# Attention into a Mish MLP on one core: weight loads by a second engine, products two slots behind, and new constants

## The chip, the cores and the metric

The kernel runs on 1 core of one Trainium2 chip. The metric is device time in microseconds (us) of one execution, and less is better. The kernel before took 982.59 us in the median of three runs (983.8, 977.85 and 982.59).

## The reference

Attention with a local window, and an MLP on what comes out of it:

```python
B, H, Sl, D = 8, 8, 512, 64      # batches, heads, local rows, head size; Sg = 32 global rows
k_all = concat([k_g, k_l]); v_all = concat([v_g, v_l])
out_g = sm(scale * q_g @ k_all.T) @ v_all              # global rows see all
s_ll = where(|row - col| <= 32, scale * q_l @ k_l.T, -1e9)
out_l = sm(concat([scale * q_l @ k_g.T, s_ll])) @ v_all
x = concat([out_g, out_l]) as rows                      # 8 * 544 = 4352 rows of 512
h = x @ w_in                                            # 512 x 2048
g = h * tanh(softplus(h))                               # Mish
return g @ w_out                                        # 2048 x 512, float32
```

## The kernel before

**The work.** Every large product is made of 16-bit floats: an operand is split into a high and a low half, and three products (high by high, high by low, low by high) stand for one.

The attention is cut into 128 *units*, one for each batch, pair of heads and quarter of the local rows; a name such as U_3_1 is batch 3, pair 1. A unit's scores `s` (line L616, TensorE) are masked and their row maxima taken by VectorE (L630), ScalarE makes the exponentials (L639) and the high half of them `ph` (L337), VectorE the low half (L659). A DMA transpose `pt<-ph` (L504, issued by SyncE) turns them, and twelve matmuls make the product `U` with the values (`va`, `vc`; L712). VectorE divides by the sums (`x`, L720 to L722), and from batch 1 on the rows are split (`xs`) and turned by DMA into `xh` and `xl`, the MLP's input; in batch 0 TensorE does the turning. Every pair of heads also has a small set of instructions for the 32 global rows (`g`, `gP`, `gu`, ...).

The MLP takes 256 rows at a time: 17 *blocks* (two for each batch, and the global rows), each of 8 *steps* i. A step makes `h` (24 matmuls, L848), Mish in ScalarE (L891), its halves `G` in VectorE (L339, L904), and adds to the output tiles `o_0` and `o_1` (six matmuls each, L916). After the eighth step ScalarE or VectorE scales `o` into `ob` (L337, L339), and a DMA stores it. PSUM holds 2 `h`, 2 `o`, 3 `s` and 1 `U`: the first `o` of a block needs the `ob` of the block before it.

**The weights** come as 64-bit floats: 32 loads of 512 KB, `w0` to `w15` for the first matrix, `w16` to `w31` for the second, all issued by GpSimd (L406, L409). VectorE makes 32-bit floats of each in three instructions (L422, L429, L431). Their scale (`w_norm`) needs all sixteen of a matrix, and then ScalarE and VectorE split each row of tiles (`W`); the second matrix's low halves are VectorE's (L493).

**The values** of a batch are one load of 1024 KB (`vraw`, one buffer). VectorE takes their maxima (`vmx`, L516 to L522), GpSimd reduces over partitions (L527), VectorE makes the scale `sv` (L531 to L535), and ScalarE and VectorE the halves (`vgf`, `vf`), which eight small DMAs of SyncE's for each pair of heads put into `va` and `vc`.

**The order.** Nothing is in program order. `slot(u)` records the tasks of unit u and of the MLP steps that the tables give to this slot; a task's place in the record is its priority (`BOOST` makes the MLP's later by that many places). The planner `Plan.order` then simulates all engines with costs of its own, each engine takes the ready task of the best priority, and that simulated order is what each engine's instructions are written in. So a constant's change reorders all engines. The constants that matter here: `BLOCKS` (slots at which the blocks 0 to 3 start), `LAGX` (how many slots each later step lies behind its number), the weights' `CONV`, `RATE`, `FIRST`, `STEP` and `AHEAD_DMA` (slots of the conversions, splits and loads).

Of the kernel before, what the change touches and what calls it, by code (L numbers as in the profile page):

```python
# [21 lines left out]
RED = bass_isa.ReduceOp  # L22
# [27 lines left out]
class Plan:  # L50
# [7 lines left out]
    LOYAL = 800  # L58
    TABLE = 1283
    COLD = 2  # L60
    DEEP, ISSUE, LANES = 4, 1000, 8

    def __init__(self):
        self.tasks = []
# [70 lines left out]
    def order(self):  # L135
        N = len(self.tasks)
        left, users = [0] * N, [[] for _ in range(N)]
        for n, t in enumerate(self.tasks):
            both = t[2] | t[3]
            left[n] = len(both)  # L140
            for d in both:
                users[d].append(n)
        free = dict.fromkeys((PE, DVE, ACT, POOL, DMA), 0)
        queue = {e: [] for e in free}
        start, done, on = [None] * N, [0] * N, [None] * N
        columns = {}
# [19 lines left out]
        def first(e):  # L166

            best = None
            for pri, n, ns, t in queue[e]:
                table = self.tasks[n][7]  # L170
                t = max(t, free[e])
                if table == "dma":
                    t = max(t, far[-self.DEEP] if len(far) >= self.DEEP else 0, soft[-self.LANES] if len(soft) >= self.LANES else 0)
                elif e == DMA:
                    t = max(t, hard[-self.LANES] if len(hard) >= self.LANES else 0)
                elif e == ACT and table not in (None, self.table):
                    t += self.TABLE
                e0 = self.tasks[n][0][0][0]
                if e0 != e and free[e0] <= t + self.LOYAL:
                    continue  # L180
                if best is None or t < best[0]:
                    best = (t, pri, e, n, ns)
                    if t == free[e]:
                        break
            return best
# [3 lines left out]
                enter(n)  # L189
        for _ in range(N):  # L190
            t, pri, e, n, ns = min(c for c in map(first, free) if c)
            start[n], on[n] = t, e
            if self.tasks[n][7] == "dma":
                s = max(t + self.DMA_IN, late)
                both = min(ns, max(0, moved + self.DMA_IN - s))
                moved += both
                late = s + ns + both
                far.append(late)
                free[e] = t + self.ISSUE
                done[n] = far[-1] + self.DMA_OUT  # L200
                soft.append(done[n])
                queue[e] = [c for c in queue[e] if c[1] != n]
                for u in users[n]:
                    left[u] -= 1
                    if not left[u]:
                        enter(u)
                continue
            if e == ACT:
                self.table = self.tasks[n][7] or self.table
            for x, _ in self.tasks[n][0]:  # L210
                queue[x] = [c for c in queue[x] if c[1] != n]
            if e == PE:
                ns = tensor(t, ns, self.tasks[n][6]) - t
            if e == DVE and free[POOL] > t:
                ns += 0.6 * min(ns, free[POOL] - t)
            if e == DMA:
                s = max(moved, t)
                both = min(ns, max(0, late - s - self.DMA_IN))
                late += both
                moved = s + ns + both  # L220
                free[e] = max(t + max(self.DMA_MIN, self.tasks[n][6]), moved - self.DMA_AHEAD)
                done[n] = moved + self.DMA_IN + self.DMA_OUT
                hard.append(done[n])
            else:
                free[e] = done[n] = t + ns
            for u in users[n]:
                left[u] -= 1
                if not left[u]:
                    enter(u)
# [15 lines left out]
def attn_mish_kernel(ctx: ExitStack, tc: tile.TileContext, qt, kt, vm, vg, qg, w1, w2, consts_in, out, w64):  # L245
# [76 lines left out]
    def dma(kib):  # L322
        return kib * 2.81
# [41 lines left out]
    def wkeys(k):  # L365
        if k < 16:
            return [[("W", k // 4 * 2 + 1 + g), k % 4] for g in range(2)]
        j, hf = HV[k]
        return [[("W", j + j // 8 + 1), hf]]
# [20 lines left out]
    def rawkey(k):  # L390
        return ("W", PLACE[k]) if PLACE[k] in range(18) else ("wraw", k)

    def word(k, w):
        x = raw(k).rearrange("p (f w) -> p f w", w=2)[:, :, w]
        return x.rearrange("p (g f) -> p g f", g=2) if k < 16 else x

    def w_load(k):
        j, hf = HV[k]

        def go():  # L400
            n = 2 if w64 else 1
            dst = raw(k) if w64 else wf(k).bitcast(I32)
            if k < 16:
                c, f0 = k % 4, k // 4 * 512 * n
                src = w1[c * 128:(c + 1) * 128, f0:f0 + 512 * n]
                G.dma_start(dst, src if w64 else src.rearrange("p (g f) -> p g f", g=2))  # L406
            else:
                r0 = (j - 8) * 256 + hf * 128
                G.dma_start(dst, w2[r0:r0 + 128, :])  # L409
        if w64:  # L410
            p = PLACE[k]
            pl.add(POOL, dma(512), go, w=[rawkey(k)] if p in range(18) else (), new=() if p in range(18) else [(p, ("wraw", k))], table="dma")
        else:
            pl.add(POOL, dma(256), go, w=wkeys(k), table="dma")

# [526 lines left out]
    UNITS.sort(key=lambda x: (x[0], x[2] // 2, x[1], x[2]) if x[0] < HALVED else x)  # L944
    steps = [(blk, i) for blk in range(NBLK) for i in range(NF)]

    BLK2 = 28.778
    BLK3 = 44.139
    LAGX = 17.0
    BLOCKS = [9, 17, max(25, int(BLK2)), max(33, int(BLK3))]  # L950
    PACE = 0.762
    S1 = [int(BLOCKS[s // NF] + PACE * (s % NF)) if s < 4 * NF else s + max(17, int(LAGX)) for s in range(len(steps))]
    LAG2 = 2
    BOOST = 78.591

    def at(u):
        return [x for x, v in zip(steps, S1) if v == u]
# [1 line left out]
    def unit(u):  # L959
        return UNITS[u] if 0 <= u < NU else None  # L960
# [3 lines left out]
    def slot(u):  # L964
# [4 lines left out]
            pl.slot = None  # L969

        m, m2, md = (at(u - k) for k in (0, LAG2, LAG2 + 1))
        fu, bu, vu = unit(u + 1), unit(u), unit(u - 1)
        b, hp, t = bu if bu else (0, 0, -1)
        n1, n3 = divmod(b * HP + hp + 1, HP), divmod(b * HP + hp + 3, HP)
        load3 = bu and b >= HALVED and HALVED < n3[0] < B
# [18 lines left out]
        for x in md:  # L994
            if x[1] == NF - 1:
                store(x[0])
        if mv1 and t == 1:
            v_hi(*n1)
        pl.late = BOOST
        for x in m[:1]:  # L1000
# [27 lines left out]
        if t == 2:  # L1028
            g_exp(b, hp)
            g_norm(b, hp)  # L1030
            g_turn(b, hp)
        if mv1 and t == 1:
            v_lo(*n1)
        pl.late = BOOST
        for x in m2:
# [13 lines left out]
        if vu and vu[0] < HALVED and vu[2] == 3:  # L1049
            k_load(vu[0] + 1, vu[1])  # L1050
            q_load(vu[0] + 1, vu[1])
        if mv1 and t == 1:
            v_move(*n1)
        if vu and vu[2] == 3 and (vu[0] < HALVED - 1 or vu[:2] == (HALVED - 1, 0)):
            v_parts(vu[0] + 1, vu[1])
# [12 lines left out]
        if bu and HALVED <= b < B - 1:  # L1068
            if hp == 2 and t == 1:
                b_load(b + 1)  # L1070
                g_load(b + 1)
            if hp == 2 and t >= 2:
                for k in ((0, 1), (2, 3, 4))[t - 2]:
                    b_max(b + 1, k)
            if hp == 2 and t == 3:
                b_scale(b + 1)
            if hp == 3 and t == 0:
                b_split(b + 1)


# [1 line left out]
    ORDER = "k0 q0 m w0 b w1 w2 k1 q1 w3 w4 k2 q2 w5 w6 k3 q3 w7 w8 w9 w10 g w11 w12 w13 w14 w15"  # L1082
    LOAD1 = -7.335
    LOADS1 = 0.0
    CONV1 = 0.623
    RATE1 = 0.077
    CONV2 = 3.656
    RATE2 = 0.645
    FIRST1 = 7.58
    STEP1 = 0.746  # L1090
    FIRST2 = 7.262
    STEP2 = 0.393
    AHEAD_DMA = 13.043

    def weights():
        for k in range(32):
# [15 lines left out]
        pl.settle()  # L1112

    V.memset(pmax, 0.0)
    pl.add(POOL, 6000, lambda: G.partition_all_reduce(warm, pmax, 128, RED.max))
    for i, x in enumerate(ORDER.split()):
        a, n = x[0], int(x[1:] or 0)
        pl.slot = LOAD1 + LOADS1 * i
# [18 lines left out]
    weights()  # L1137
    splits += [(FIRST1 + STEP1 * j, j) for j in range(8)] + [(FIRST2 + STEP2 * j, 8 + j) for j in range(8)]
    splits.sort()
    for u in range(-1, max(S1[-1] + LAG2 + 2, NU + 2)):  # L1140
        slot(u)
    with tc.manual_schedule(engines={E.PE, E.DVE, E.Activation, E.Pool, E.SP}):
        pl.emit()
# [55 lines left out]
```

## Time and profile before

| | |
|---|---|
| runs | 983.8, 977.85, 982.59 us; median 982.59 us |
| profiled execution | 984.26 us, span 982.3 us |
| TensorE busy (matmuls) | 920.9 us, 94% of the span |
| VectorE, ScalarE busy | 570.0 us and 573.5 us, 58% each |
| GpSimd busy | 29.8 us |
| mean granted TensorE clock | 0.982 |
| DMA | 113.74 MB, mean 116 GB/s |

The span runs from the first to the last instruction; the execution's own time has 1.96 us around it. Engines are PE (TensorE), DVE (VectorE), ACT (ScalarE), POOL (GpSimd) and SP (SyncE, which issues most DMAs). A clock of 1.00 is 2.4 GHz, of 0.50 it is 1.2 GHz. A row such as "9.5, 8, 1.9" in the view of the waits gives the total, the count and the longest wait.

### The profile page before, as it was taken

To read this page: it belongs to the slowest core of one execution; us is meant where nothing else is said; L and a number is where in the kernel's file an instruction comes from. 1 tells how busy PE (TensorE), PEld (TensorE's weight loads), DVE (VectorE), ACT (ScalarE), POOL (GpSimd) and SP (SyncE) were. 2 spreads that over 40 slices of the span, in tenths; PEclk is the share of its full clock that TensorE was granted. 3 is DMA by queue.
4 is the path that set the end of the run, shared out by engine and by line. 5 is a ranking of instruction groups with operands and counts; after the bars stand their busy time and mean duration, and the time that the engine had idled before them with its cause. 6 is when DMAs were issued, how large, how long until landed. Compare 5 with 4: busy or idle time off the path is not lost.

```text
span 982.3 us, 20578 instructions
## 1 busy us (share of the span) xinstructions
PE 920.9 (94%) x8044; PEld 627.1 (64%) x8044; DVE 570.0 (58%) x1747; ACT 573.5 (58%) x1181; POOL 29.8 (3%) x57
## 2 busy tenths in 40 slices
PE   2678899999899879999999999999999999999997
PEld 1456556767566556667676667666666666666664
DVE  4799886667477554766566655665565553322222
ACT  2266876778578556767676767676776753211111
POOL 6201000000000000000000000000000000000000
PEclk9689999999999999999999999999999999999999
DMA  9874225676677844567356555646362333000000
GB/s 360 299 220 135 87 62 135 125 148 150 157 147 148 176 119 103 119 149 146 84 132 144 122 105 125 154 88 132 93 121 48 83 63 62 22 1 22 1 22 22
DMA packets 214417, 113.74 MB, mean 116 GB/s; under 512 B 181168, under 2 KB 194608, under 8 KB 213296
## 3 DMA queue, kind: packets, MB, share of 16 engines
q1 hardware_dynamic: 209568, 95.39, 43.6%
q0 software_dynamic: 4608, 16.78, 4.8%
q8 instruction: 63, 1.03, 0.4%
q14 instruction: 34, 0.28, 0.1%
q10 hardware_dynamic: 144, 0.26, 0.1%
HBM read 46.32 MB, written 8.91 MB: 56 GB/s over the span
## 4 chain that ended last, share of the span: by engine, by line
PE 77%; DMA 7%; DVE 7%; ACT 5%; SPq 1%; issue 1%; POOL 1%; ACTq 0%; DVEq 0%; POOLq 0%
PE h L848 31%; PE o L916 31%; PE s L616 5%; PE U L712 4%; DMA pt<-ph 3%; PE g L750 2%; DMA vraw<-in_vm 1%; PE gu L804 1%; PE rest L487 1%; ACT L891 1%; DVE W L429 1%; DVE W L431 1%; DMA va<-vgf 1%; ACT P L639 1%; DVE G L904 1%
## 5 line engine op out<-in xcount | busy, mean ns | idle before, releaser
L916 PE MATMUL o<-W,G 128*128 128x512 f16 x1632 | 388.7, 380 | 5.3 <-ACT ob L337 5.3
L848 PE MATMUL h<-xh,W 128*128 128x256 f16 x2048 | 376.2, 273 | 2.5 <-ACT W L330 2.5
L848 PEld LDWEIGHTS <-W 128*128 128x128 f16 x3264 | 310.0, 98 | 69.5 <-issue 9.3
L848 PE MATMUL h<-xl,W 128*128 128x256 f16 x1024 | 279.7, 273 | 0.0
L916 PEld LDWEIGHTS <-G 128*128 128x128 f16 x1632 | 156.3, 98 | 155.9 <-issue 10.3
L891 ACT ACTIVATE e<-h,c 128x512 f32<-128x512 f32 (+1 forms) x137 | 92.4, 684 | 161.9 <-PE h L848 137.4
L339 DVE TENSOR_SCALAR G<-e,c 128x512 f16<-128x512 f32 x135 | 64.8, 482 | 169.4 <-ACT e L891 168.2
L639 ACT ACTIVATE P<-P,nm 128x192 f32<-128x192 f32 (+1 forms) x256 | 117.4, 459 | 63.2 <-DVE nm L630 61.6
L904 DVE SCALAR_TENSOR_TENSOR G<-e,c,G 128x512 f16<-128x512 f32 (+1 forms) x137 | 101.7, 745 | 3.4
L630 DVE CUSTOM_DVE_ANT_0 P<-s,consts 128x192 f32<-128x192 f32 (+1 forms) x256 | 86.1, 368 | 27.8 <-PE s L616 24.5
L712 PEld LDWEIGHTS <-pt 96*128 96x128 f16 (+1 forms) x1536 | 61.0, 98 | 40.3 <-DMA pt<-ph 14.9
L891 ACT ACT_TABLE_LOAD x65 | 83.4, 1283 | 1.1
L659 DVE SCALAR_TENSOR_TENSOR ph<-P,ph 128x384 f16<-128x384 f32 (+1 forms) x112 | 63.7, 588 | 30.9 <-ACT ph L337 28.6
L712 PE MATMUL U<-va,pt 128*128 128x64 f16 (+1 forms) x768 | 56.7, 194 | 18.4 <-DMA pt<-ph 9.5
L616 PE MATMUL s<-k,q 64*128 64x192 f32 (+1 forms) x512 | 66.2, 375 | 4.9 <-DMA q<-in_qt 4.6
L337 ACT ACTIVATE ph<-P 128x384 f16<-128x384 f32 (+1 forms) x107 | 54.9, 537 | 12.7 <-DMA pt<-ph 12.2
L616 PEld LDWEIGHTS s<-k,q 64*128 64x128 f32 x512 | 44.3, 194 | 22.5 <-issue 14.8
L712 PE MATMUL U<-vc,pt 96*128 96x64 f16 x768 | 56.0, 194 | 0.0
L772 ACT ACT_TABLE_LOAD x25 | 32.1, 1283 | 40.4 <-DVE gmx L767 40.3
L639 ACT ACT_TABLE_LOAD x40 | 51.3, 1283 | 0.7
L639 ACT ACTIVATION_READ_ACCUMULATOR P<-P,nm 128x1 f32 x256 | 47.8, 187 | 0.0
L337 ACT ACTIVATE ob<-o,c 128x512 f32<-128x512 f32 (+1 forms) x34 | 22.8, 669 | 29.4 <-PE o L916 29.4
(116 smaller groups left out, 714.1 us busy)
## 6 DMA issues: line engine op xcount, KB each, us to landing
k<-in_kt SPq DMA_DIRECT2D x32, 320.0 KB, 3.6
wraw<-in_w POOLq DMA_DIRECT2D x17, 512.0 KB, 9.2
out<-ob SPq DMA_DIRECT2D x33, 256.0 KB, 2.4
q<-in_qt SPq DMA_DIRECT2D x32, 256.0 KB, 2.9
vraw<-in_vm SPq DMA_DIRECT2D x8, 1024.0 KB, 6.1
W<-in_w POOLq DMA_DIRECT2D x15, 512.0 KB, 7.8
vc<-vf SPq DMA_DIRECT2D x32, 128.0 KB, 2.5
va<-vf SPq DMA_DIRECT2D x32, 96.0 KB, 2.7
```

The source lines that it names most:

```text
L337: A.activation(out=dst, in_=src, func=AF.Copy, scale=c)
L339: V.tensor_scalar(dst, src, c, None, ALU.mult)
L616: T.matmul(X[s[h]][:, cols(u)], X[q][r, u * 128:(u + 1) * 128], X[k][r, c0:c0 + w], start=True, stop=True)
L630: pl.add(DVE, 155 + 1.04 * w, lambda: V.tensor_tensor_reduce(out=half(P, h, w), in0=X[s][:, cols(t)], in1=mask[:, m0:m0 + w], scale=-SCALE ...
L639: pl.add(ACT, 460, lambda: A.activation(out=half(P, h, w), in_=half(P, h, w), func=AF.Exp, bias=X[nm], scale=-1.0, accum_out=X[sums][:, t, ...
L659: pl.add(DVE, dve(n), lambda: V.scalar_tensor_tensor(p_part(X[ph], t, 1), p_src(X[P], t), PSC, p_part(X[ph], t, 0), ALU.mult, ALU.subtract ...
L712: T.matmul(X[u][:, t, h, :], X[pt][:k, p * 4 + h * 2 + c, :], X[vx][:k, t, vl, h * 64:(h + 1) * 64], start=(n == 0), stop=(n == 5))
L772: pl.add(ACT, 470, lambda: A.activation(out=X[P], in_=X["g", b, hp][:, :272], func=AF.Exp, bias=X[mx][:, 2:3], scale=SCALE, accum_out=X[s] ...
L848: T.matmul(X[h][:, f * TB:(f + 1) * TB], wh(i, wl)[:, off:off + 128], X[x][:, d, o:o + TB], start=(n == 0), stop=(n == 11))
L891: chain(blk, i, ACT, 705, lambda a, z: A.activation(out=X[e][:, a:z], in_=hv(blk, i)[:, a:z], func=AF.Mish, bias=0.0, scale=X[c][:, 0:1]), ...
L904: chain(blk, i, DVE, 668, lambda a, z: V.scalar_tensor_tensor(gp(1, blk, i)[:, a:z], X[e][:, a:z], X["c", blk][:, 2:3], gp(0, blk, i)[:, a ...
L916: T.matmul(X[o], gp(g, blk, i)[:, f, t * 128:(t + 1) * 128], wh(8 + i, wl)[:, f * 512:(f + 1) * 512], start=(i == 0 and n == 0), stop=(i = ...
```

## The change

1. The loads of `w0` to `w4` are issued by ScalarE instead of GpSimd.
2. From unit 24 on the product with the values, and what follows from it (x and its turns), is recorded two slots after its unit instead of one; the MLP's smallest lag of later steps becomes 18 slots instead of 17.
3. From batch 2 on the next values' maxima, scale and split are recorded two to one slots later, and the halves and moves for the next batch's first pair of heads (`v_hi`, `v_lo`, `v_move`) one slot later.
4. Constants: block 2 starts at slot 29 instead of 28, block 3 at 39 instead of 44, later steps lie 19 slots behind instead of 17, `BOOST` is larger, and the weights' places are new. In the planner, DMA issues cost 450 (ScalarE) and 600 (GpSimd) instead of 1000, GpSimd is busy until 6900 ns, ScalarE's loads share the eight hardware lanes with SyncE's, and VectorE is not taken to be slower while GpSimd issues DMAs.

```diff
+    FIRST_ACT = 5
+
     def w_load(k):
...
-                G.dma_start(dst, src if w64 else src.rearrange("p (g f) -> p g f", g=2))
+                (nc.scalar if k < FIRST_ACT else G).dma_start(dst, src if w64 else src.rearrange("p (g f) -> p g f", g=2))
...
-    BLK2 = 28.778
-    BLK3 = 44.139
-    LAGX = 17.0
+    BLK2 = 29.322
+    BLK3 = 39.967
+    LAGX = 19.225
     BLOCKS = [9, 17, max(25, int(BLK2)), max(33, int(BLK3))]
-    PACE = 0.762
-    S1 = [int(BLOCKS[s // NF] + PACE * (s % NF)) if s < 4 * NF else s + max(17, int(LAGX)) for s in range(len(steps))]
+    PACE = 0.79
+    S1 = [int(BLOCKS[s // NF] + PACE * (s % NF)) if s < 4 * NF else s + max(18, int(LAGX)) for s in range(len(steps))]
     LAG2 = 2
-    BOOST = 78.591
+    LATER = 24
+    BOOST = 84.4
...
-        fu, bu, vu = unit(u + 1), unit(u), unit(u - 1)
+        fu, bu, vu = unit(u + 1), unit(u), unit(u - 1) if u - 1 < LATER else unit(u - 2) if u - 2 >= LATER else None
...
-        if mv1 and t == 1:
+        if mv1 and t == (2 if hp == 3 else 1):
             v_hi(*n1)
...
-            if hp == 2 and t >= 2:
-                for k in ((0, 1), (2, 3, 4))[t - 2]:
+            if hp == 2 and t == 3:
+                for k in range(3):
                     b_max(b + 1, k)
-            if hp == 2 and t == 3:
+            if hp == 3 and t == 0:
+                for k in (3, 4):
+                    b_max(b + 1, k)
                 b_scale(b + 1)
-            if hp == 3 and t == 0:
+            if hp == 3 and t == 1:
                 b_split(b + 1)
...
-    CONV1 = 0.623
-    RATE1 = 0.077
-    CONV2 = 3.656
-    RATE2 = 0.645
-    FIRST1 = 7.58
-    STEP1 = 0.746
-    FIRST2 = 7.262
-    STEP2 = 0.393
-    AHEAD_DMA = 13.043
+    CONV1 = -1.386
+    RATE1 = 0.0
+    CONV2 = 2.335
+    RATE2 = 0.495
+    FIRST1 = 6.564
+    STEP1 = 1
+    FIRST2 = 6.491
+    STEP2 = 0
+    AHEAD_DMA = 12.164
```

**ScalarE at the start of the program.** The names are the loads' landing tiles (`wraw`, `W`) and the first exponentials `P`. Before:

```order
L253 ACT_TABLE_LOAD
L639 ACTIVATE P_74,sums_0_0_139<-P_74,nm_0_0_0_134 128x192
L639 ACTIVATE P_74,sums_0_0_139<-P_74,nm_0_0_1_141 128x192
L639 ACTIVATE P_75,sums_0_0_139<-P_75,nm_0_1_0_151 128x224
L639 ACTIVATE P_75,sums_0_0_139<-P_75,nm_0_1_1_163 128x224
L337 ACTIVATE dv_199<-consts,sv_186 128x128
```

and in the changed kernel:

```order
L257 ACT_TABLE_LOAD
L412 DMA wraw_99<-in_w 128x1024
L412 DMA wraw_101<-in_w 128x1024
L412 DMA wraw_105<-in_w 128x1024
L412 DMA wraw_108<-in_w 128x1024
L412 DMA W<-in_w 128x1024
L645 ACTIVATE P_74,sums_0_0_147<-P_74,nm_0_0_0_138 128x192
```

Five loads now stand between the table load and the first exponential.

**VectorE between the first values' maxima `vmx` and the end of their scale `sv`.** `W<-wraw` and `W<-W` are steps of weight conversions. Before:

```order
L522 TENSOR_REDUCE vmx_145<-vmx_145 128x1
L431 SCALAR_TENSOR_TENSOR W<-wraw_103,W 128x2x256
L422 TENSOR_SCALAR W<-wraw_108 128x2x256
L422 TENSOR_SCALAR W<-wraw_110 128x2x256
L531 TENSOR_SCALAR p_0_170<-p_0_170 128x1
L343 TENSOR_SCALAR p_0_170<-p_0_170 128x1
L346 TENSOR_SCALAR sv_186<-p_0_170 128x1
```

and in the changed kernel:

```order
L437 SCALAR_TENSOR_TENSOR W<-wraw_108,W 128x2x256
L522 TENSOR_REDUCE vmx_171<-vraw_110 128x1 x3
L526 TENSOR_REDUCE vmx_171<-vgraw_122 128x1
L428 TENSOR_SCALAR W<-W 128x2x256
L528 TENSOR_REDUCE vmx_171<-vmx_171 128x1
L726 TENSOR_SCALAR rs_0_0_190<-sums_0_0_147 128x4
L435 SCALAR_TENSOR_TENSOR W<-W 128x2x256
L727 RECIPROCAL rs_0_0_190<-rs_0_0_190 128x4
L437 SCALAR_TENSOR_TENSOR W<-W 128x2x256
L537 TENSOR_SCALAR p_0_201<-p_0_201 128x1
L347 TENSOR_SCALAR p_0_201<-p_0_201 128x1
L350 TENSOR_SCALAR sv_210<-p_0_201 128x1
```

The five weights whose loads ScalarE issues are now all converted ahead of the scale; before, two whole weights and the first step of two more were.

**ScalarE around the output tiles `ob_3` of block 3**, which free the two `o` that block 4 needs. Before:

```order
L891 ACT_TABLE_LOAD
L891 ACTIVATE e_4_1_4556<-h_4_1_4479,c_4_2770 128x512
L543 ACTIVATE vgf_4_4617<-vgraw_4_2039,sv_4_4597 128x2x128
L337 ACTIVATE vf_4_0_4619<-vraw_4_4435,sv_4_4597 128x4x128
L891 ACTIVATE e_4_2_4631<-h_4_2_4569,c_4_2770 128x512
L337 ACTIVATE ob_3_4644<-o_3_0_3802,c_3_1989 128x512
L772 ACT_TABLE_LOAD
L772 ACTIVATE gP_3_1_4656,gs_3_1_4657<-g_3_1_4558,gmx_3_1_4582 128x272
L639 ACTIVATE P2_76,sums_3_2_4675<-P2_76,nm_3_2_0_0_4667 128x192
L639 ACTIVATE P2_76,sums_3_2_4675<-P2_76,nm_3_2_0_1_4678 128x192
L337 ACTIVATE ob_3_4644<-o_3_1_3815,c_3_1989 128x512
```

and in the changed kernel:

```order
L549 ACTIVATE vgf_4_4372<-vgraw_4_1941,sv_4_4344 128x2x128
L778 ACTIVATE gP_3_0_4378,gs_3_0_4379<-g_3_0_4327,gmx_3_0_4340 128x272
L645 ACTIVATE P1_75,sums_3_1_4383<-P1_75,nm_3_1_0_0_4376 128x192
L341 ACTIVATE ob_3_4399<-o_3_0_3856,c_3_1909 128x512
L645 ACTIVATE P1_75,sums_3_1_4383<-P1_75,nm_3_1_0_1_4385 128x192
L645 ACTIVATE P2_76,sums_3_1_4383<-P2_76,nm_3_1_1_0_4401 128x224
L645 ACTIVATE P2_76,sums_3_1_4383<-P2_76,nm_3_1_1_1_4406 128x224
L341 ACTIVATE ph0_80<-P1_75 128x4x96
L341 ACTIVATE ph1_81<-P2_76 128x2x224
L334 CAST xs_3_0_4472<-x_3_0_4467 128x512
L341 ACTIVATE ob_3_4399<-o_3_1_3866,c_3_1909 128x512
L897 ACT_TABLE_LOAD
```

Both `ob_3` now stand ahead of block 4's first Mish (`e_4_0` follows the table load); before they stood behind its second and third. `vgf_4`, which waits for the scale of batch 4's values, is ahead of `ob_3` in both.

## Rows read from the trace of the kernel before

**Rows 1.** Windows: stretch; length, busy us (instructions) by engine, PE clock, DMA share, GB/s.

```profile
0.00:50.00 50.00, 21.99 (x139) 14.56 (x139) 30.62 (x81) 13.16 (x31) 21.56 (x41) 0.83 0.91 328
8.00:32.00 24.00, 9.75 (x55) 5.82 (x56) 17.88 (x50) 9.17 (x23) 10.47 (x20) 1.00 1.04 401
50.00:125.00 75.00, 62.90 (x524) 42.48 (x524) 67.03 (x208) 53.66 (x112) 5.86 (x11) 0.91 0.48 145
125.00:325.00 200.00, 191.68 (x1848) 131.60 (x1847) 139.91 (x468) 145.86 (x330) 0.94 (x2) 1.00 0.64 136
325.00:375.00 50.00, 42.39 (x388) 27.91 (x386) 25.70 (x80) 27.76 (x60) 0.35 (x1) 0.97 0.67 144
375.00:700.00 325.00, 324.93 (x2962) 223.05 (x2960) 196.52 (x623) 223.10 (x447) 1.05 (x3) 1.00 0.55 121
```

**Rows 2.** Timeline, 0 to 8 us: start, length, engine, line, tiles.

```profile
0.72 1.28 ACT L253 ACT_TABLE_LOAD   x1 [0.72 <-PEq L1188]
...
6.89 1.23 POOL L406 DMA_DIRECT2D wraw<-in_w  x2
```

**Rows 3.** Timeline of VectorE, 8 to 46 us; in brackets its idle time before and the releaser.

```profile
13.70 0.43 DVE L422 TENSOR_SCALAR W<-wraw 128x512 int32<-128x512 int32 x1 [12.85 <-DMA wraw<-in_w]
...
22.33 0.15 DVE L535 TENSOR_TENSOR pmax<-pmax,p 128x1 f32<-128x1 f32 x1
...
28.24 0.75 DVE L422 TENSOR_SCALAR W<-W 128x512 int32<-128x512 int32 x2
...
31.32 0.68 DVE L683 SCALAR_TENSOR_TENSOR pt<-PT,pt 128x512 f16<-128x512 f32 x1
...
43.02 0.43 DVE L722 TENSOR_TENSOR x<-U,rs 128x256 f32<-128x256 f32 x1 [5.31 <-PE U L712]
```

**Rows 4.** DMA issues of the first 44 us: tiles, issuer, count, size, median us to landing.

```profile
vraw<-in_vm SPq DMA_DIRECT2D x1, 1024.0 KB, 6.3
...
consts<-in_consts SPq DMA_DIRECT2D x1, 176.0 KB, 3.3
```

**Rows 5.** Chain of work that ended last: start, length, piece.

```profile
6.89 6.78 DMA wraw<-in_w
...
33.04 8.03 DMA va<-vgf
...
360.36 1.31 PE h L848 x12
...
363.34 2.59 PE o L916 x12
```

**Rows 6.** Timeline, 113 to 123 us: first low half of the second matrix, first output product.

```profile
118.26 1.28 DVE L493 SCALAR_TENSOR_TENSOR W<-W,sw 128x1024 f16<-128x1024 f32 x1
...
121.70 1.67 PE L916 MATMUL o<-W,G 128*128 128x512 f16 x7
```

**Rows 7.** Waits of the whole span: who waited for what: total us, times, longest.

```profile
DVE vmx L516 <- DMA vraw<-in_vm: 12.1, 6, 3.9
...
PE U L712 <- DMA pt<-ph: 9.5, 8, 1.9
```

**Rows 8.** Timeline, 333 to 360 us.

```profile
340.27 1.28 DVE L516 TENSOR_REDUCE vmx<-vraw 128x1 f32<-128x512 f32 x2 [3.94 <-DMA vraw<-in_vm]
...
348.25 0.51 ACT L543 ACTIVATE vgf<-vgraw,sv 128x256 f16<-128x256 f32 x1 [2.79 <-DVE sv L347]
...
349.85 0.67 ACT L337 ACTIVATE ob<-o,c 128x512 f32<-128x512 f32 x1
...
350.58 4.21 PE L916 MATMUL o<-W,G 128*128 128x512 f16 x12 [2.46 <-ACT ob L337]
...
358.55 1.45 PE L916 MATMUL o<-W,G 128*128 128x512 f16 x6 [2.86 <-ACT ob L337]
```

**Rows 9.** DMA queue of SyncE, 275 to 350 us: packets, MB, share of the 16 engines.

```profile
q1 hardware_dynamic: 28486, 12.00, 79.7%
```

**Rows 10.** The same queue, 500 to 575 us.

```profile
q1 hardware_dynamic: 22331, 10.17, 61.6%
```

More of the change, by code (lines that the diff above doesn't have):

```diff
@@ L60 @@
     COLD = 2
-    DEEP, ISSUE, LANES = 4, 1000, 8
+    DEEP, ISSUE, SOFT, LANES = 4, 450, 600, 8
     def __init__(self):
@@ L143, in order @@
         free = dict.fromkeys((PE, DVE, ACT, POOL, DMA), 0)
+        free[POOL], pool = 6900, "dma"
         queue = {e: [] for e in free}
@@ L172, in first @@
                 if table == "dma":
-                    t = max(t, far[-self.DEEP] if len(far) >= self.DEEP else 0, soft[-self.LANES] if len(soft) >= self.LANES else 0)
+                    lane = hard if e == ACT else soft
+                    t = max(t, far[-self.DEEP] if len(far) >= self.DEEP else 0, lane[-self.LANES] if len(lane) >= self.LANES else 0)
                 elif e == DMA:
@@ L191, in order @@
             t, pri, e, n, ns = min(c for c in map(first, free) if c)
+            if e == POOL:
+                pool = self.tasks[n][7]
             start[n], on[n] = t, e
@@ L198, in order @@
                 far.append(late)
-                free[e] = t + self.ISSUE
+                free[e] = t + (self.ISSUE if e == ACT else self.SOFT)
                 done[n] = far[-1] + self.DMA_OUT
-                soft.append(done[n])
+                (hard if e == ACT else soft).append(done[n])
                 queue[e] = [c for c in queue[e] if c[1] != n]
@@ L213, in order @@
                 ns = tensor(t, ns, self.tasks[n][6]) - t
-            if e == DVE and free[POOL] > t:
+            if e == DVE and free[POOL] > t and pool != "dma":
                 ns += 0.6 * min(ns, free[POOL] - t)
@@ L411, in w_load @@
             p = PLACE[k]
-            pl.add(POOL, dma(512), go, w=[rawkey(k)] if p in range(18) else (), new=() if p in range(18) else [(p, ("wraw", k))], table="dma")
+            pl.add(ACT if k < FIRST_ACT else POOL, dma(512), go, w=[rawkey(k)] if p in range(18) else (), new=() if p in range(18) else [(p, ("wraw", k))], table="dma")
         else:
-            pl.add(POOL, dma(256), go, w=wkeys(k), table="dma")
+            pl.add(ACT if k < FIRST_ACT else POOL, dma(256), go, w=wkeys(k), table="dma")
     def w_bits(k):
@@ L1031, in slot @@
             g_turn(b, hp)
-        if mv1 and t == 1:
+        if mv1 and t == (2 if hp == 3 else 1):
             v_lo(*n1)
@@ L1051, in slot @@
             q_load(vu[0] + 1, vu[1])
-        if mv1 and t == 1:
+        if mv1 and t == (2 if hp == 3 else 1):
             v_move(*n1)
@@ L1114, in attn_mish_kernel @@
     V.memset(pmax, 0.0)
-    pl.add(POOL, 6000, lambda: G.partition_all_reduce(warm, pmax, 128, RED.max))
+    pl.add(POOL, 600, lambda: G.partition_all_reduce(warm, pmax, 128, RED.max))
     for i, x in enumerate(ORDER.split()):
@@ L1139, in attn_mish_kernel @@
     splits.sort()
-    for u in range(-1, max(S1[-1] + LAG2 + 2, NU + 2)):
+    for u in range(-1, max(S1[-1] + LAG2 + 2, NU + 3)):
         slot(u)
```

## The prediction

> **What bounds the kernel now.** I read the windows first. TensorE is busy 324.93 of the 325 us from 375 to 700, so whatever is late there on other engines costs nothing. Before 375 it is busy 21.99 of the first 50 us, 62.90 of the next 75, 191.68 of the next 200 and 42.39 of the next 50 [rows 1]: 28.0 + 12.1 + 8.3 + 7.6 = 56.0 us without a matmul, and part of the first 125 us is at a granted clock below 1.00 besides. TensorE's instructions are the same in number before and after (no matmul is added or removed), so every microsecond of idleness taken out before 375 comes off the end, and one put in is added. The change can win or lose only there, and I take four places one after the other.
>
> **The start** is a matter of loads and of VectorE. The first weight load is issued by GpSimd at 6.89, though ScalarE's only instruction, the table load, is over at 0.72 + 1.28 = 2.00 [rows 2]. The load takes 6.78 us [rows 5], and VectorE starts at 13.70 after 12.85 us of idleness [rows 3]. The values' scale is done at 22.33 + 0.15 = 22.48, and the first `x` waits until 43.02, because the moves of the values (`va<-vgf`, 8.03 us as the chain has it) land only then [rows 3, 5]. From 8 to 32 us the DMA share is 1.04 at 401 GB/s: the queues are full [rows 1].
>
> **Edit 1: five loads by ScalarE.** ScalarE loses the time of five issues, which lies ahead of its first exponential and waits for scores and row maxima anyway: nothing. The first load can go out at 2.0 instead of 6.89. If it took the 6.78 us of the row it would land at 8.8; by the sizes in the start's DMA view (176 KB 3.3 us, 1024 KB 6.3 us [rows 4]) 512 KB would take some 4.5 us and land at 6.5, and the 3.3 us of the small one is the floor (5.3). I take 8.0, nearer to the row of the load itself. But the change also puts more conversions ahead of the scale. Counted with the durations of this trace (two weights take 31.32 - 28.24 = 3.08 us, so 1.54 each [rows 3]), VectorE's work from its first conversion to the end of the scale is 8.4 us before (it took 22.48 - 13.70 = 8.8) and 12.6 after. So the scale comes at 8.0 + 12.6 + 0.4 = 21.0 instead of 22.5, not five microseconds sooner. The moves then join full queues. GpSimd's own issues still begin at 6.89, now with the sixth weight, so each later load stands five issues (0.6 us each by [rows 2]) further ahead in its queue, but in a DMA that is full anyway. The bytes ahead of the moves are the same, and the extra 4.9 us of loading share the DMA with SyncE's own; I let the first `x` gain 0.3 (bounds 0 and 4.4, the latter with the floor of the load).
>
> What the lead buys comes later. VectorE is busy 67.03 of the 75 us from 50 to 125 [rows 1] and so the engine that sets the pace there. Counted in the same way, its work from the first `x` to the first low half of the second matrix (which needs all 32 weights) is 69.0 us before, where it took 118.26 - 43.02 = 75.2 [rows 3, 6], and 63.3 after: the conversions that were done in the gap at the start are missing (-2.1), a row maximum (-0.8), a pair's work for the global rows (-2.3) and a `G` (-0.5). That is -5.7. Not all of it need reach TensorE: the first `o` at 121.70 stands more than a microsecond behind that low half, behind hidden-layer matmuls [rows 6]. **Start: -5 us** (bounds 0 and -10.1, which is 5.7 + 4.4).
>
> **The output tiles of block 3.** Around 350 two stalls stand one behind the other. ScalarE's `ob` waits in order behind `vgf`, `vgf` waited 2.79 us for the scale of batch 4's values, that for maxima which waited 3.94 us for the load `vraw`; so TensorE's first `o` of block 4 waits 2.46 us, its twelve matmuls then take 4.21 where 2.59 is usual, and the second output tile costs another 2.86 [rows 5, 8]. Together 2.46 + 1.62 + 2.86 = 6.9 us, nearly all of the 7.6 us that TensorE lost from 325 to 375 [rows 1].
>
> **Edits 2 to 4 there.** In the changed order both `ob_3` stand ahead of block 4's first Mish instead of behind its second and third, and TensorE has 9.3 us of other work between the last `o_3` and the first `o_4` (counted with the prices of twelve `h` and `o`, 1.31 and 2.59 [rows 5]); before, block 4's first `o` stood ahead of the last matmuls into `o_3_1` and 1.3 us of work behind those into `o_3_0`. `vgf_4` still stands ahead of `ob_3`, so the wait for `vraw` remains, but 9.3 us is more than its 2.79. **-6 us** (bounds -2.9, where only one of the two goes, and -6.9).
>
> **The turned exponentials.** TensorE waited for `pt<-ph` eight times, 9.5 us in all, 1.9 at the longest [rows 7]; nearly all of it lies between 245 and 345, where SyncE's queue takes 79.7% of the DMA engines against 61.6% later [rows 9, 10]. From unit 24 on the product now comes two slots behind its unit. That is worth less than it sounds, since the planner had set the distances: TensorE's work between a unit's scores and its product, counted with the same prices, was under 13 us in 9 of the 32 units of batches 2 and 3, and is in 6 of the 32 after; from batch 4 on it grows from 13.5 or more to 15 or more, where nothing waits anyway. The densest stretch (ten units in 34.6 us of TensorE's work) becomes one of six units in 20.7, a like density but shorter. **-4 us** (bounds 0 and -9.5).
>
> **What is late next.** The rows `x` of batch 2, which block 4 needs, are later by the same slot. On VectorE the low half of that batch's last `xs` now stands behind the first maximum of `vmx_4`, and so behind the load `vraw`: such maxima waited 12.1 us in six times, 3.9 at the longest [rows 7]. TensorE's work between the last product of batch 2 and `h_4_0` is 12.1 us against 11.9, so there is no more cover than before. **+1 us** (bounds 0 and +3.9).
>
> Making the values' scale and its first moves later by one to two slots costs nothing by itself from batch 4 on: TensorE does not idle there.
>
> **Sum.** -5 - 6 - 4 + 1 = -14 us. The profiled execution took 984.26 us (span 982.3 and 2.0 around it); -14 makes 970.3. It is 1.7 above the median of the runs shown, so the median to expect is **968.6, or 969 us**. All terms at their good ends give -10.1 - 6.9 - 9.5 = -26.5, a median of 956.
>
> **Rivals.**
>
> *The stalls only move.* The crowd of attention units ahead of block 4 is now squeezed into fewer slots (block 3 starts at slot 39, not 44), and the turns still go through one queue at 79.7%. Then the 6 and 4 us come back as waits elsewhere before 375 but for some 2; with the start's 5 that is -7 + 1 = -6: 976.6. For it: the planner's old order was also free of waits by its own count, and the trace has 9.5 us of them. Against it: the stall at 350 has a cause that the new order takes away.
>
> *The start gains nothing.* The queues are full from 8 to 32 us [rows 1]; five more loads in them before 7 us delay `k`, `q` and `vraw`, and as SyncE's issues now share their lanes with ScalarE's, its third to sixth loads wait for earlier ones to land. Then VectorE starts earlier but its scale, 4.2 us of work further away, is not earlier at all, and the 5.7 us shrink with it: -9, 973.6. The Trainium skill ("DMA: Bandwidth & Descriptors", section "Issuing engines are not separate DMA queues") says that DMAs run on the same 16 engines whichever engine started them, and that issuing from several saves only the sequencer's time. By that rule the start would give 0 and the sum would be 973.6. The trace agrees as to the full queues (1.04), but here it was not the issue's length but its time, 6.89, that was late. The rule has no say on that.
>
> *Slower.* Twelve products, those of pairs 1 to 3 of batch 3, have their turns in the squeezed stretch beside block 4's first steps. If each waits w us for its `pt<-ph`, the 4 us are not gained and 12 w are added: 982.6 - 10 + 12 w. From w = 0.83 on it is slower than before, from 1.65 on by more than 1%; at 2.0 it is 996.6. Against it: 1.9 was the longest single wait, not the mean [rows 7], and the mean of eight was 1.2.
>
> *It does not do what it says:* the order drifts from the plan at the first late landing, and the gains at 350 and at the start are lost in other waits: within 3 us of 982.6.
>
> **Chances.** Forecast 0.52 (its own range 960 to 973), the stalls only move 0.17, no gain at the start 0.13, nothing 0.10, slower place 0.08 (nearly half of it under 992). The range from 956 to 983 leaves out the slow case, part of "nothing" and a tail below. A measurement of this kernel tells about 1%, 9.8 us, from no change: faster means under 972.8, slower above 992.4. Of the forecast 0.47 lies under 972.8, and of the next two rivals 0.13 together: 0.60 faster; 0.05 slower; 0.35 in between.
>
> **What would show it.** VectorE's first conversion at about 8 us and the first scale at about 21; the first `x` within a microsecond or two of 43; the first `o` near 116. Between 325 and 375 no wait of `o` for `ob`, and TensorE busy over 47 of 50 us. Waits of `U` for `pt<-ph` of at most 6 us in the whole span. A gap of at most 4 us ahead of `h_4_0`. I am wrong if the first conversion is early and the first `o` is not (then VectorE's lead is lost in waits), if waits for `pt<-ph` cluster in batch 3, or if TensorE idles after 400, which would make a term out of what I cost at nothing.

## The result, and the profile after

The changed kernel takes 966.43 us in the median of four runs (964.78 to 970.07), against 981.77 for the kernel before (977.85 to 983.8): a ratio of 0.9854 (95% interval 0.981 to 0.9898), 15 us faster. Forecast were 969 us, a range of 956 to 983, and 0.6 for faster by over 1%. The profiled execution took 970.07 (span 968.3, the slowest of the four), 14.2 below that of before; the sum said -14. But two of its terms had the right size without the reason that it gave, as the experiments show.

The windows of the changed kernel, in the columns of [rows 1]:

```profile
0.00:50.00 50.00, 20.92 (x136) 13.17 (x137) 32.29 (x84) 13.04 (x32) 16.93 (x33) 0.86 0.83 303
8.00:32.00 24.00, 13.29 (x77) 7.90 (x73) 21.77 (x63) 9.77 (x27) 8.00 (x15) 1.00 1.03 402
50.00:125.00 75.00, 64.94 (x551) 43.41 (x552) 67.51 (x208) 54.41 (x113) 7.52 (x14) 0.98 0.53 160
125.00:325.00 200.00, 194.30 (x1842) 132.02 (x1842) 138.00 (x453) 139.03 (x316) 1.00 (x2) 0.99 0.67 142
325.00:375.00 50.00, 48.15 (x502) 34.64 (x501) 37.58 (x133) 39.42 (x92) 0.35 (x1) 1.00 0.81 158
375.00:700.00 325.00, 325.00 (x2980) 223.39 (x2979) 197.12 (x627) 218.60 (x443) 1.06 (x3) 1.00 0.57 123
```

TensorE is busy 1.1 us less in the first 50, then 2.0, 2.6 and 5.8 us more, and never idle from 375 to 700: as before, all is decided ahead of 375. These 9.3 us of idleness are not the whole gain. Over the whole span the same matmuls take 916.2 us instead of 920.9, because less of them runs at 1.2 GHz (the granted clock is 0.98 instead of 0.91 from 50 to 125): 4.7 of the 14.0 us by which the spans differ.

VectorE's timeline at the start and at the second matrix, and the first `o` (answers to [rows 3] and [rows 6]):

```profile
5.54 1.01 DVE L428 TENSOR_SCALAR W<-wraw 128x512 int32<-128x512 int32 x1 [4.69 <-DMA wraw<-in_w]
...
21.31 0.15 DVE L541 TENSOR_TENSOR pmax<-pmax,p 128x1 f32<-128x1 f32 x1
...
44.62 0.42 DVE L728 TENSOR_TENSOR x<-U,rs 128x256 f32<-128x256 f32 x1 [9.92 <-PE U L718]
...
113.90 1.28 DVE L499 SCALAR_TENSOR_TENSOR W<-W,sw 128x1024 f16<-128x1024 f32 x1 [0.44 <-ACT W L341]
...
116.13 4.21 PE L922 MATMUL o<-W,G 128*128 128x512 f16 x15
```

The first conversion starts 8.2 us earlier, the scale is done at 21.46 instead of 22.48, the first `x` comes 1.6 us *later*, and yet the first `o` 5.6 us earlier, with the same 646 matmuls of TensorE's ahead of it. Windows up to the first `o`, before and after:

```profile
0.00:121.70 121.70, 81.59 (x647) 55.51 (x647) 95.11 (x285) 64.00 (x140) 27.42 (x51) 0.87 0.66 221
```

```profile
0.00:116.13 116.13, 76.99 (x647) 52.42 (x647) 91.78 (x272) 59.95 (x132) 24.45 (x46) 0.93 0.66 224
```

So 4.6 of the 5.6 us are the same matmuls at a higher clock, and 1.0 is idleness. Why the first `x` is late stands in the chain of waits:

```profile
22.74 0.41 DVE vgf L551
23.15 0.02 issue
23.17 11.88 DMA vgraw<-in_vg
35.05 0.02 issue
35.06 8.03 DMA va<-vgf
43.10 0.04 issue
43.14 1.45 PE U L718 x24
```

A move of the first pair's values goes out at 35.06, when a load of batch 2's `vgraw` lands that was issued at 23.17 and is first read at 156. The DMAs of SyncE and ScalarE take eight lanes in turn, and one does not go out before the last DMA of its lane has landed; this move is the eighth issue after that load, and the load took 11.88 us in a DMA that is full.

The lane is the smaller part of it, though. In every trace here SyncE's DMAs landed in the order in which they were issued. The first of the moves, which no lane held, went out at 25.48 and landed only at 36.09, behind that load; the move before the one at 35.06 went out at 32.67 and landed at 42.71, only 0.4 us ahead of it. What stood ahead of all the moves in SyncE's queue were its own loads, `k` and `q` of the third and fourth pair among them: in the kernel before these two pairs' loads went out from 4.23 us on, here, where ScalarE's loads take lanes too, from 12.21 on.

The waits of the whole span:

```profile
DVE vmx L522 <- DMA vraw<-in_vm: 7.2, 5, 3.0
...
PE U L718 <- DMA pt<-ph: 5.2, 4, 2.1
...
PE gu L810 <- DMA gpt<-gph: 2.0, 4, 0.7
```

The waits for turned exponentials fall from 9.5 to 5.2 us; those of the global rows (`gpt`) rise from 0.8 to 2.0. No wait of `o` for `ob` is left. The timeline around it (answer to [rows 8]):

```profile
326.03 2.75 PE L922 MATMUL o<-W,G 128*128 128x512 f16 x12
...
327.17 0.51 ACT L549 ACTIVATE vgf<-vgraw,sv 128x256 f16<-128x256 f32 x1 [6.03 <-DVE sv L351]
...
328.84 0.68 ACT L341 ACTIVATE ob<-o,c 128x512 f32<-128x512 f32 x1
...
333.63 0.68 ACT L341 ACTIVATE ob<-o,c 128x512 f32<-128x512 f32 x1
...
340.14 1.46 PE L922 MATMUL o<-W,G 128*128 128x512 f16 x6
```

ScalarE's `vgf` still waits for the scale of batch 4's values, 6.03 us now instead of 2.79; but that wait is over at 327.17, before the last products into `o_3` end at 328.78, and TensorE wants the freed `o` only at 340.14, 5.8 us after the second `ob` is through. So nobody feels it.

### The profile page after: what moved, and what is told of

Same layout as the page of the kernel before. It is cut to its first block, busy times and chain, and to the rows that moved or that the text cites. A ratio compares the mean times of both kernels' runs of the same rounds, so it can differ in the third digit from the quotient of the medians.

```text
span 968.3 us, 20568 instructions
## 1 busy us (share of the span) xinstructions
PE 916.2 (95%) x8044; PEld 624.2 (64%) x8044; DVE 569.8 (59%) x1747; ACT 555.7 (57%) x1163; POOL 26.9 (3%) x52
## 4 chain that ended last, share of the span: by engine, by line
PE 81%; DMA 7%; DVE 6%; ACT 3%; SPq 1%; issue 1%; POOL 0%; ACTq 0%
PE h L854 34%; PE o L922 33%; PE s L622 5%; PE U L718 4%; PE g L756 2%; PE gu L810 2%; DMA gpt<-gph 1%; DMA vgraw<-in_vg 1%; DMA pt<-ph 1%; PE rest L493 1%; DMA xl<-xs 1%; DMA va<-vgf 1%; DMA wraw<-in_w 1%; DVE W L437 1%; SPq L330 1%
## 5 line engine op out<-in xcount | busy, mean ns | idle before, releaser
L341 ACT ACTIVATE ph<-P 128x384 f16<-128x384 f32 (+1 forms) x99 | 51.3, 539 | 12.2 <-DMA pt<-ph 11.4
```

The costliest lines, as they stand in the source:

```text
L341: A.activation(out=dst, in_=src, func=AF.Copy, scale=c)
```

## The experiments

All ran in five rounds beside the kernel before, and are given as medians with the ratio to it. "Every instruction in its place" means that the planner's order was kept and only what the diff shows was done to it.

**1. Who issues the loads.** In the changed kernel, back to GpSimd; in the kernel before, `w0` to `w4` to ScalarE; the order of both kept.

```diff
-                (nc.scalar if k < FIRST_ACT else G).dma_start(dst, ...)
+                G.dma_start(dst, ...)
```

> The changed kernel with every instruction in its place, but w0 to w4 are issued by GpSimd again (after its memsets, near 6.9 us). Theory A (the early loads give the start its 4.8 us): VectorE's first conversion goes from 5.5 back to about 13.7, the first scale from 21.5 to 13.7 + 12.6 + 0.4 = 26.7, and some 5 us more are lost at the first o; 966.4 + 5 = 971, and up to 974 if the scale's reduction queues behind GpSimd's loads. Rival B (the new constants' order gives it, and the early loads are lost in the wait for the values' moves, 9.9 us before the first x): within 1 us of 966.4, and the first x within 1 us of 44.6.

> The kernel before with every instruction in its place, but w0 to w4 are issued by ScalarE. Theory A (early loads alone are worth the start's gain): first conversion near 5.5 instead of 13.7, first scale 3 to 6 us earlier, first o 3 to 5 us earlier than 121.7, time 981.8 - 4 = 978. Rival B (the old order has nothing to put into the time gained, and the moves of the values wait for lanes and full queues): first x still at 43 or later, time within 1.5 us of 981.8.

The first took 968.05 us (0.9867, 0.9849 to 0.9886), 1.6 above the changed kernel; the second 984.88 (1.0046, 1.003 to 1.0062), slower than the kernel before. Their first `x`, from VectorE's timeline of the two kernels apart:

```profile
46.55 0.43 DVE L728 TENSOR_TENSOR x<-U,rs 128x256 f32<-128x256 f32 x1 [5.96 <-PE U L718]
```

```profile
46.53 0.42 DVE L722 TENSOR_TENSOR x<-U,rs 128x256 f32<-128x256 f32 x1 [10.67 <-PE U L712]
```

With GpSimd's loads the first conversion is back at 13.96, the first `x` is 1.9 us later, and the first `o` at 116.62, only half a microsecond later. So the early loads don't give the start its 5 us: that is nearest to rival B of the first expectation, though both the time (1.6 us off, where it said 1) and the `x` moved more than it said. In the second, the scale was ready at 17.42, five microseconds early, and the `x` still came 3.5 us later than before. Two things used up the lead. TensorE stood in order behind the second pair's scores, whose `q` was issued at 5.57 and took 13.79 us; and then the moves landed late. The chain of this kernel, and a move of the kernel before:

```profile
5.57 13.79 DMA q<-in_qt
19.35 0.14 issue
19.49 1.76 PE s L616 x8
21.24 2.00 PE VT L570 x2
...
24.32 12.28 DMA va<-vf
36.60 0.02 issue
36.62 7.97 DMA va<-vgf
```

```profile
26.49 6.53 DMA va<-vf
```

`VT` makes the low halves of the first values, which the moves need. So of the five microseconds at the scale only 2.2 are left when the first move goes out (24.32 instead of 26.49). It then takes 12.28 us to land instead of 6.53, and that turns the lead into a loss: SyncE's own loads, which share their lanes with ScalarE's now, are still on their way (the last one ahead of it lands at 35.75).

**2. Which constants give the start.** The kernel before with the weights' nine constants alone; the changed kernel with the blocks' old constants. Both are planned anew.

```diff
-    CONV1 = 0.623
+    CONV1 = -1.386
...
-    BLK3 = 39.967
-    LAGX = 19.225
+    BLK3 = 44.139
+    LAGX = 17.0
```

> The kernel before with the nine constants of the weights alone (CONV, RATE, FIRST, STEP, AHEAD_DMA), planned anew; loads stay with GpSimd, the planner's costs as before. Theory A (these constants give the start's 4.8 us): first x at 43 as before, first low half of the second matrix near 114 instead of 118.3, first o near 116 to 117: 981.3 - 4.5 = 977. Rival B (the planner's new costs of issues, lanes and GpSimd are needed too): within 1.5 us of 981.3.

> The changed kernel with the old constants of the blocks (BLK2, BLK3, LAGX, PACE, BOOST; the later steps lie 18 slots behind, the least that the new products allow), planned anew; loads by ScalarE, the weights' constants and the planner's new costs stay. Of the start (TensorE's lost time from 75 to 125 us, 17.6 us before, 12.3 after): theory A, the weights' constants with the planner's new costs give it, 12 to 13 stay; rival B, the blocks' constants give it, 16 to 18. Of the middle, by either: products of batch 2 have only 7 to 9 us of work behind their scores and ob_3 stands behind vgf_4 again with 3 us between o_3 and o_4, so the waits for turns rise to 9 or more and up to 6 us of waits for ob come back. Time 966.4 + 8 = 974 by A, 979 by B.

The weights' constants alone: 983.85 (1.0022, 1.0004 to 1.004), no gain, as in rival B, though 1 us beyond its bound. The first `o` did come early, at 113.88, but with 580 matmuls ahead of it instead of 646, so its time alone does not tell the gain. The blocks' old constants: 970.44 (0.9885, 0.9865 to 0.9905). Windows from 75 to 125 us, of the kernel before, the changed one, the one with GpSimd's loads, the one with the weights' constants and the one with the old blocks:

```profile
75.00:125.00 50.00, 43.51 (x359) 29.85 (x358) 43.08 (x123) 38.01 (x66) 4.63 (x8) 0.94 0.39 114
```

```profile
75.00:125.00 50.00, 47.37 (x392) 32.72 (x393) 44.49 (x137) 39.39 (x74) 3.35 (x6) 0.97 0.36 101
```

```profile
75.00:125.00 50.00, 46.76 (x418) 32.91 (x417) 44.48 (x137) 39.70 (x77) 3.36 (x6) 1.00 0.40 104
```

```profile
75.00:125.00 50.00, 45.70 (x368) 29.79 (x365) 43.51 (x123) 37.33 (x70) 3.24 (x6) 0.90 0.36 99
```

```profile
75.00:125.00 50.00, 47.35 (x393) 32.46 (x390) 44.69 (x136) 38.74 (x73) 3.35 (x6) 0.97 0.38 99
```

TensorE's 3.9 us more, at a higher clock, are there whoever issues the loads and whatever the blocks' constants; the weights' constants without the planner's new costs give a half of them, at a clock of 0.90, and lose as much earlier (the first `x` at 50.65). So, by elimination, the start's gain is the new order of conversions and splits, and the weights' constants do not make it without the planner's new costs. Whether the costs make it without the constants is open: they weren't tried alone. Of the middle, the expectation of experiment e11 failed: no wait of `o` for `ob` came back, and the waits for turns were 5.6 us, where 9 or more were expected. Where its 4 us lie the traces don't show: its profiled execution took 970.77, only 0.7 above that of the changed kernel; TensorE is busy 2.4 us less from 125 to 325 and 1.9 more from 325 to 375.

**3. The stall at 350 us.** In the kernel before, both `ob_3` were put right behind their products in ScalarE's order: the first ahead of `vgf_4` and the first `vf_4` (shown here), the second ahead of the two exponentials in front of it; and, planned anew, the lag of the later steps alone was made 19.

```diff
 L891 ACTIVATE e_4_1
+L337 ACTIVATE ob_3<-o_3_0
 L543 ACTIVATE vgf_4
 L337 ACTIVATE vf_4_0
 L891 ACTIVATE e_4_2
-L337 ACTIVATE ob_3<-o_3_0
```

> The kernel before with ScalarE's order changed at one place: the first output tile ob_3 of block 3 goes ahead of batch 4's vgf and first vf (which wait for the scale of batch 4's values); all else keeps its order. Theory A (the stall of TensorE at 350 us is ScalarE standing in order behind that scale): the 2.46 us wait of o for ob and the slow twelve products behind it go, -3 to -5 us: 977 to 979; the second wait of 2.86 us stays. Rival B (TensorE's stall only moves to the next late thing, the turned exponentials or the moves of batch 4's values): within 1 us of 981.8.

> The kernel before with LAGX = 19.225 alone, planned anew: blocks from the fourth on two slots later. The order up to block 3 is the same; ob_3 now stands ahead of vgf_4, with 8 us of TensorE's work between the last o_3 and the first o_4; but two products of batch 3 have only 4.2 us of work behind their scores. Theory A (the lag is what ends the stall of o for ob, and the attention units it leaves bare wait for their turns instead): no wait of o for ob (-7), waits of products for turns 9.5 + 8 = 17 or more: 981 to 984, no gain. Rival B (the stall at 350 just goes, -5 to -7): 975 to 977.

The first: 976.73 (0.9946, 0.9926 to 0.9966), theory A; the second: 995.28 (1.0151, 1.0123 to 1.018). Two output tiles that stood behind other work in one engine's queue were worth 4.6 us. From the timeline of the first:

```profile
346.86 0.69 ACT L354 ACTIVATE ob<-o,c 128x512 f32<-128x512 f32 x1 [1.38 <-PE o L937]
...
347.97 2.75 PE L937 MATMUL o<-W,G 128*128 128x512 f16 x12
...
352.48 1.46 PE L937 MATMUL o<-W,G 128*128 128x512 f16 x6 [0.85 <-ACT ob L354]
```

The twelve products take 2.75 instead of 4.21. The second wait has shrunk as well, from 2.86 to 0.85, where the expectation had it stay: it left out that the edit moves the second `ob_3` too (351.75 instead of 357.83), so the 4.6 us are not the first wait's alone. With the lag alone the wait for `ob` is gone too, but products that are left with 4.2 us of work behind their scores wait for their turns (15.7 us in all, 4.3 at the longest). It is 11 us worse than theory A had it. The stretch around 350 runs at a slow clock, and TensorE is no longer free of waits behind 375. Those (6.3 us) are for the turned rows of the global set, whose waits of the whole span stand behind the two windows:

```profile
325.00:375.00 50.00, 40.20 (x375) 27.12 (x374) 33.34 (x115) 34.43 (x80) 0.51 (x1) 0.86 0.84 159
375.00:700.00 325.00, 318.71 (x2888) 218.84 (x2887) 185.58 (x584) 217.96 (x427) 1.06 (x3) 1.00 0.57 117
```

```profile
PE gu L804 <- DMA gpt<-gph: 7.7, 5, 2.9
```

That is the mechanism of the forecast's slower rival, brought about by the lag alone. Which edit takes the stall at 350 out of the changed kernel is not settled by this: with the old blocks' constants (e11) no wait for `ob` came back either.

**4. The second slot, and the values' scale.** The changed kernel with the product one slot behind throughout, and with the old places of the values' maxima, scale and split; planned anew.

```diff
-    LATER = 24
+    LATER = 1000
```

> The changed kernel with LATER = 1000, planned anew: the product with the values is one slot behind its unit throughout. TensorE's work between scores and product is under 12 us in 17 of the 64 units of batches 2 and 3 taken pairwise (down to 7.2), against 9 in the changed kernel, and block 3's output tiles stay ahead of block 4. Theory A (the second slot is what shortens the waits for turned exponentials): these waits go from 5.2 to 9 us or more, 970 to 973. Rival B (block 3's earlier start and the longer lag give the distance): within 1.5 us of 966.4.

> The changed kernel with the values' maxima, scale, split and first moves recorded where they were before, planned anew. Theory A (this edit costs and gains nothing by itself): within 2 us of 966.4. Rival B (it keeps maxima that wait for the load of the values out of VectorE's way): waits of VectorE for that load rise above 7.2 us, 969 or more.

One slot: 973.83 (0.9929, 0.9904 to 0.9953), 7.4 us above the changed kernel. That is nearly theory A's time (0.8 above its range), but not by its mechanism: the waits for `pt` are 5.6 us where 9 or more were expected, hardly more than the 5.2 with two slots. One of them is 3.55, and its window, with that of the changed kernel behind it, shows the rest (a clock of 0.86 is a mean of time at 2.4 and at 1.2 GHz):

```profile
282.92 0.34 PE L718 MATMUL U<-va,pt 128*128 128x64 f16 x3 [3.55 <-DMA pt<-ph]
```

```profile
275.00:300.00 25.00, 20.51 (x176) 14.74 (x175) 15.63 (x48) 17.10 (x43) 0.00 (x0) 0.86 0.70 134
```

```profile
275.00:300.00 25.00, 25.00 (x269) 19.37 (x267) 16.77 (x57) 18.75 (x43) 0.00 (x0) 1.00 0.66 143
```

The window has 4.5 us of idleness, and its mean clock is 0.86 where the changed kernel has 1.00. The old places of the values: 966.71 (0.9841, 0.9816 to 0.9866), no difference, theory A: that edit is worth nothing.

**5. The loads ahead of the moves.** The three loads (`vgraw` of batches 1 and 2, `qg` of batch 1) behind the moves of the first two pairs' values in SyncE's order, all else kept: in the changed kernel, in the kernel before, and in the changed kernel with GpSimd's loads or with only three by ScalarE.

```diff
 qg_0
-vgraw_1
-qg_1
-vgraw_2
 va_0_0 ... vc_0_1, va_0_1
+vgraw_1
+qg_1
+vgraw_2
 va_0_2
```

> The changed kernel with SyncE's order changed at one place: three loads that are needed much later (vgraw of batches 1 and 2, qg of batch 1) go behind the moves of the first two pairs' values; all else keeps its order. Theory A (the move that ends the wait of the first x stood in a lane behind the load of batch 2's vgraw, 11.9 us to land): the first x comes 4 to 8 us before 44.6, VectorE's 9.9 us of idleness shrink by as much, and 2 to 6 us of it reach the end: 960 to 964. Rival B (the DMA is full until then, so the moves land no earlier, or VectorE's lead is lost again before the first o): within 1 us of 966.4.

> The kernel before with SyncE's same three loads behind the moves of the first two pairs' values; all else keeps its order. Theory A (there too the last move of the first pair stands in a lane behind such a load): first x 2 to 5 us earlier than 43.0 and 2 to 5 us off the end, 976 to 979. Rival B (there the moves are held by the full DMA, not by a lane): first x within 1 us of 43.0, time within 1.5 us of 981.2.

> The kernel with SyncE's three loads behind the moves (958.5 us with ScalarE's loads), every instruction in its place, but w0 to w4 are issued by GpSimd. With GpSimd's loads the changed kernel took 968.1, first x at 46.55, and SyncE issued the first pair's moves without the long lane wait. Theory A (the early loads are worth their five to six microseconds once no lane of SyncE's stands between them and the first x): first x at 45 to 46.5, 965 to 968, that is 7 to 9 us above the same order with ScalarE's loads. Rival B (the order of the moves alone gives the gain): first x at 39 to 41, 958 to 961.

> The kernel with SyncE's three loads behind the moves (958.5 us), every instruction in its place, but w3 and w4 are issued by GpSimd, so that ScalarE issues three loads. Theory A (the queue of the second pair's q, 14 us from issue to landing, is what TensorE stands behind ahead of the values' halves, and fewer weights ahead of it let it land earlier): q lands 2 to 4 us earlier, the moves go out 1 to 2 us earlier, 956 to 958. Rival B (the scale at 20.8 holds the moves, or w3 and w4 come late for VectorE): 958 to 961.

| SyncE's order | `w0` to `w4` by GpSimd | by ScalarE |
|---|---|---|
| kernel before | 981.3 | 984.9 |
| kernel before, loads behind | 982.4 | not tried |
| changed kernel | 968.05, first `x` 46.55 | 966.43, first `x` 44.62 |
| changed kernel, loads behind | 967.28, first `x` 45.80 | **958.51, first `x` 39.33** |

958.51 (0.978, 0.9763 to 0.9797) is faster than both kernels and more than theory A expected of it: all of the 5.3 us at the first `x` reach the end, and some more. With GpSimd's loads the same order took 967.28 (0.986, 0.9835 to 0.9884), theory A. Three by ScalarE gave 959.49 (0.9786, 0.9759 to 0.9812), rival B; in the kernel before the same order did nothing (1.0007, 0.999 to 1.0024), since there the first move landed after 6.53 us anyway and the next ones waited for it. Neither edit gives more than 2 us alone, both together 9.5 (968.05 - 958.51): the early loads were worth having, but loads for later batches in SyncE's queue kept them. The first move of the changed kernel, and with the three loads behind (KB, us from issue to landing):

```profile
va<-vf SPq DMA_DIRECT2D x1, 32.0 KB, 10.6
```

```profile
va<-vf SPq DMA_DIRECT2D x1, 32.0 KB, 6.4
```

It goes out at 25.48 and at 25.04, held by no lane in either, and lands 4.6 of the 5.3 us earlier. So the three loads' own place in the queue explains most of the gain, and the lane at most the 0.7 us that are left; no run changes the lanes alone. The best kernel's first `x` and first `o`:

```profile
39.33 0.42 DVE L740 TENSOR_TENSOR x<-U,rs 128x256 f32<-128x256 f32 x1 [5.15 <-PE U L730]
```

```profile
109.30 2.98 PE L934 MATMUL o<-W,G 128*128 128x512 f16 x13
```

## Why the prediction was right, and where not

**What bounds it**: right as to the place: TensorE's busy time behind 375 hardly changes (324.93 and 325.00 of 325 us). But the sum counted idleness, and of the clock only the slow products at 350; 4.7 of the 14.0 us are matmuls that take less time at a higher clock.

**Edit 1 and the start, -5**: right in size, wrong in cause. The first `o` came 5.6 us earlier (forecast near 116, measured 116.13). Two steps failed. "The change also puts more conversions ahead of the scale" was right, but its 21.0 (measured 21.46) was luck: the first conversion came 2.5 us earlier than taken, and the way from it to the end of the scale took 15.9 us instead of 13.0, in part because ScalarE's fourth load waited for its lane until 7.01 and landed at 14.38 (1.7 us of VectorE's time). "I let the first `x` gain 0.3" was a loss of 1.6: I had counted queues that are full, and not that SyncE's own loads would go out later and land ahead of the moves. And "what the lead buys comes later" tied the 5.7 us of VectorE's work to the early loads. The work did shrink (from the first `x` to the first low half 69.3 us instead of 75.2), but with GpSimd's loads nearly all of the gain stays (1.6 us apart), so it is the order's; and it reached TensorE mostly as a higher clock (4.6 of 5.6 us up to the first `o`). The rival "the start gains nothing" was wrong on the time and right on the mechanism: shared lanes and full queues took what edit 1 gave. By the rule of the Trainium skill cited there ("DMA: Bandwidth & Descriptors", section "Issuing engines are not separate DMA queues") another issuer saves only the sequencer's time. In the kernel before it gained nothing (984.88 against 981.32); with the three loads behind the moves it gained 8.8 us (967.28 - 958.51), where the loads also went out six microseconds earlier, on which the rule has no say.

**The output tiles, -6**: right. Both waits (5.3 us) and the slow products (1.6) are gone; the wait for the scale, 6.03, was over before the last `o_3` was made. Moving the two `ob_3` alone is worth 4.6.

**The turned exponentials, -4**: right in size, 9.5 to 5.2, but not shown to come from the second slot, to which the forecast tied it: without it these waits are 5.6, and with the blocks' old constants 5.6 too. What takes them down stays open. The second slot matters all the same (7.4 us), more than "worth less than it sounds" had it: without it one wait is longer, and its window has a lower clock.

**What is late next, +1**: not there. TensorE shows no wait at `h_4_0`, and VectorE's waits for `vraw` fell to 7.2. In its place the global rows' turns cost 1.2.

By rows: -5.6 (first `o`) - 4.3 (`pt`) - 6.9 (`ob`) + 1.2 (`gpt`) = -15.6, where the profiled times differ by 14.2. The 1.4 between them I have not traced. One thing on record is of that size, the clock of another stretch, 1.00 before and 0.93 after; that is 1.75 us of the 25 by an estimate from the two rows:

```profile
250.00:275.00 25.00, 23.15 (x211) 14.48 (x210) 12.55 (x41) 12.51 (x26) 0.35 (x1) 1.00 0.63 148
```

```profile
250.00:275.00 25.00, 22.90 (x182) 13.03 (x181) 15.37 (x51) 13.04 (x31) 0.65 (x1) 0.93 0.79 173
```

## What to carry to other kernels

A transfer that is issued long before it is needed can cost more than one issued late: where the DMAs of one queue land in the order of issue, look for a small move that stands behind a load for later. The chain of waits names what released the move; whether that was also the cause is seen from a move that nothing held. Two edits that are each worth less than 2 us can be worth nearly ten together, so undo them in pairs, with the order held, before one is given up. In an order made by a planner the effect of a constant is read from the resulting order, and the work that covers a wait can be counted there.

## What the runs showed of the hardware that was not expected

ScalarE's loads went out during its table load, from 0.75 us, not behind it at 2.00, and VectorE worked on the first from 5.54, where I had taken 8.0. In the full DMA of the start a load of 256 KB took 13.79 us and one of 128 KB 11.88, against a median of 2.9 for such a `q` over the whole span of the kernel before. All 586 DMAs of SyncE landed in the order of issue, in each of the traces, so that a move of 32 KB took 10.6 or 6.4 us by what was issued ahead of it. And the 25 us around a single wait of TensorE of 3.55 us had a granted clock of 0.86, so that it went with a loss larger than its length.
